# Leftover pairs of a two-layer expert product: weights of the first product held in the array, second product over half blocks

## The chip, the cores and the metric

The kernel runs on one core of a Trainium2 chip. A core has a matrix engine (TensorE, "PE"; its loads of the held operand are listed apart as "PEld"), a vector engine (VectorE, "DVE"), a scalar engine (ScalarE, "ACT"), GpSimd ("POOL") and a sync engine ("SP") that issues most DMAs. The metric is the device time of one execution in microseconds, the median of several. A "held" or "stationary" operand is the one a matmul loads into the array; the "moving" one streams past it.

## The reference, cut to what matters

An attention block makes 4608 token rows of 512 numbers, a dense gated layer maps each row to a new one, and then every token goes to one of 8 experts:

```python
logits = x @ w_gate                                  # x: (4608, 512)
e_idx = np.argmax(logits, axis=1)                    # one expert per token
eom = 1.0 / (1.0 + np.exp(-(x @ w_output_gate)))
for e in range(8):
    mask = e_idx == e
    h = np.maximum(x[mask] @ w1[e], 0.0)             # w1[e]: (512, 1024)
    ye = h @ w2[e]                                   # w2[e]: (1024, 512)
    out[mask] = gate_w[mask, None] * eom[mask, e, None] * ye
```

The change is in this last part alone, and there only in the tokens that are left over once whole blocks are taken.

## The kernel before, in words

The first 670 us compute the attention, the dense layer and the routing: rows are sorted by expert into a DRAM table `xs`, and a second table `tab` holds, for each sorted place, the token's number and its output factor. Then come two kinds of work, in an order written out by hand (`ORDER`):

- 16 **slots**. A slot takes up to 256 rows of one expert (`slot`, `gemm1`, `gemm2e`). Its products are made in three matmuls each from operands split into a rounded part and a rest, with the splitting on ACT (lines 1061, 1073) and DVE (1061, 1074). A slot's second products run one step late: they wait in `pend`, and `drain` issues them.
- **pairs**, for what is left. A pair takes two units of at most 64 rows each, mostly of two different experts, and works in unsplit float32. 11 pairs are in the program; three run always (before the sixth slot, before the tenth and at the end), and the eight behind them stand under nested conditions at the end, each taken only if there are that many units. With these inputs three run.

In a **pair** (line 1420), the two units share the array by column groups of 64: unit 0 uses columns 0 to 63 and PSUM partitions 0 to 63, unit 1 the others (`tile_position=(0, 64 * i)`). `pair1` (1028) holds the 64 rows of a unit, transposed, and streams 256 columns of its `w1` past them; a chunk is 4 such steps over the 512 inputs for each unit, and there are four chunks. Between chunk 0 and chunk 1 the last slot's waiting second products are issued (`drain(0)`). Two chunks fill one PSUM bank; ACT applies relu to it (`pair_relu`, 1036). The second product needs h with its features on the partitions, so `pair_turn` (1041) transposes it: four PE transposes by an identity (line 1044) into a PSUM bank, and a DVE copy (1046). `pair2` (1049) then holds 64 columns of the turned h and streams 512 columns of `w2`, eight steps for each unit. `finish` (1096) scales the bank on ACT (1104) and scatters its 128 rows of 2 KB to `out` with one indirect DMA issued by POOL (1107).

A float32 matmul of the program stands in the trace as two matmuls and two loads.

Weights come by DMAs that SP issues in program order (`load_weights`, 931): four of 512 KB for `w1` and four for `w2`, per unit or slot. SP has eight DMA semaphores which it uses in turn, so a DMA is issued once the one eight places earlier has landed. For slots and late pairs a DMA is skipped where the same expert's weights already lie there. `load_own` (959) fetches token numbers and factors, for a pair by two small DMAs.

Of the kernel before, what the change touches and what calls it, by code (L numbers as in the profile page):

```python
# [8 lines left out]
F32 = mybir.dt.float32  # L9
R32 = mybir.dt.float32r  # L10
B16 = mybir.dt.bfloat16
U32 = mybir.dt.uint32
AF = mybir.ActivationFunctionType
ALU = mybir.AluOpType
# [5 lines left out]
DM, DF = 512, 2048  # L20
NE, EF = 8, 1024
SEQ = NQ + NS
NX, NT = NB * NQ, NB * SEQ
# [59 lines left out]
def tile_kernel(  # L83
# [15 lines left out]
    nc = tc.nc  # L99
    V, S, G, T, D = nc.vector, nc.scalar, nc.gpsimd, nc.tensor, nc.sync  # L100
# [3 lines left out]
    def pool(c, name, bufs=1, side=None, space=None):  # L104
        kw = {"space": space} if space else {}
        return c.enter_context(tc.tile_pool(name=name, bufs=bufs, side=side, reuse_waits="tile", **kw))

    actx, nctx = ExitStack(), ExitStack()
    cp = pool(ctx, "cp", side="left")
    mp = pool(ctx, "mp", 2, side="left")  # L110
    wp = pool(nctx, "wp", side="left")
    np_ = pool(nctx, "np", side="left")
    ap = pool(actx, "ap", 2, side="right")
# [5 lines left out]
    tab = tc.dram_tile([NTAB, 2], U32, name="tab")  # L119
    half0 = tc.dram_tile([128, 4, DM], F32, name="half0")  # L120

    def psum(tag, bufs=1):
        return pp.tile([128, 512], F32, tag=tag, name=tag, bufs=bufs)

    ident = cp.tile([128, 128], F32, name="ident")
# [3 lines left out]
    def C(name):  # L129
        o, n = off[name]  # L130
        return cst[:, o:o + n]
# [6 lines left out]
    num, start = [cp.tile([128, 2 * NE], F32, name=t) for t in ("num", "start")]  # L138
    x1h = cp.tile([128, 4, 2 * 128], R32, name="x1h")
    x1l = cp.tile([128, 4, 2 * 128], R32, name="x1l")  # L140
    gap = cp.tile([128, 8], F32, name="gap")

    woh, wol = {}, {}
    win = [np_.tile([128, 4, 512], F32, name=f"win{c}") for c in range(4)]
# [3 lines left out]
    def not_yet(i):  # L148

        tc.add_manual_dep(i.ins, marks[-1].name, LATER, reason="has time")  # L150
# [396 lines left out]
    placed, put, first_placed, first_put = [], [], [], []  # L547

    sooner, later_rows = [], []

    def apart(i, mine, others):

        for o in others:
            tc.declare_no_dep(i, o, reason="rows of earlier batches")
        mine.append(i)

    def after(i, others):
        for o in others:
            tc.add_manual_dep(i, o.name, DEP, reason="token numbers in place")
# [364 lines left out]
    ws = {}  # L924

    def open_streams(qs, n0):
        for i in range(n0, n0 + 2):
            ws[i] = ([qs.tile([128, 4, 256], F32, name=f"w1s{i}{c}") for c in range(4)],
                     [qs.tile([128, 2, DM], F32, name=f"w2s{i}{c}") for c in range(4)])

    def load_weights(i, e_ap, need_ap):
        e = D.value_load(e_ap, min_val=0, max_val=NE - 1)
        kw = {}
        if need_ap is not None:
            kw["cond"] = D.value_load(need_ap, min_val=0, max_val=1)
        for k in range(2):
            for c in range(4):
                t = ws[i][k][c]
                src = (w1, w2)[k]
                D.dma_start(t.rearrange("p a f -> p (a f)"), src[bass.ds(e * 128, 128), 1024 * c:1024 * c + 1024], **kw)  # L940

    qa = {}
# [16 lines left out]
    def load_own(bases, n, placed):  # L959

        own = cp.tile([128, 2, 2], U32, tag="own", name="own", bufs=5)
        for j, reg in enumerate(bases):
            base = D.value_load(reg, min_val=0, max_val=NTAB - n)
            if n == 64:
                i = D.dma_start(own[64 * j:64 * j + 64, 0, :], tab[bass.ds(base, n), :]).ins
            else:
                i = D.dma_start(own, tab[bass.ds(base, n), :].rearrange("(t p) w -> p t w", p=128)).ins
            after(i, placed)
            if placed is first_placed:
                apart(i, sooner, later_rows)  # L970
        return own

    got_first, last_turned, last_w, evicted = [], [], [], []
# [29 lines left out]
        return xh, xl  # L1003

    zeros = {}

    def zero_tails(j0, j1):

        if j0 == 0:
            zeros["z"] = mp.tile([128, DM], F32, tag="xr", name="zeros", bufs=2)  # L1010
            V.memset(zeros["z"], 0.0)
            pair = carry.rearrange("p (j two) -> p two j", two=2)
            ends, zeros["at"] = one("ends", NE // 2), one("tails", NE // 2, U32)
            V.tensor_tensor(ends, pair[:, 1, :], pair[:, 0, :], op=ALU.subtract)
            V.scalar_tensor_tensor(ends, ends, C("half"), pair[:, 0, :], op0=ALU.mult, op1=ALU.add)
            V.tensor_scalar(zeros["at"], ends, C("part64"), None, op0=ALU.add)
        new = []
        for j in range(j0, j1):
            i = G.indirect_dma_start(xs, bass.IndirectOffsetOnAxis(ap=zeros["at"][:, j:j + 1], axis=0), zeros["z"], None).ins
            tc.add_manual_dep(i, last_w[0].name, DEP, reason="in its time")  # L1020
            apart(i, later_rows, sooner)
            for o in new:
                tc.declare_no_dep(i, o, reason="places are distinct")
            after(i, put)
            new.append(i)
        put.extend(new)

    def pair1(ps, c, x):

        for k in range(4):  # L1030
            for i in range(2):
                o = slice(64 * i, 64 * i + 64)
                T.matmul(ps[o, 256 * (c % 2):256 * (c % 2) + 256], x[:, k, o], ws[2 + i][0][c][:, k, :],
                         start=(k == 0), stop=(k == 3), tile_position=(0, 64 * i))

    def pair_relu(ps):
        h = mp.tile([128, 512], F32, tag="gh", name="hr", bufs=3)
        S.activation(h, ps, AF.Relu)
        return h

    def pair_turn(h):
        ps = psum("misc", 2)
        for k in range(4):
            T.transpose(ps[:, 128 * k:128 * k + 128], h[:, 128 * k:128 * k + 128], ident)
        hT = mp.tile([128, 4, 128], F32, tag="gl", name="hT", bufs=3)
        V.tensor_copy(hT.rearrange("p k t -> p (k t)"), ps)
        return hT

    def pair2(py, ft, hT):
        for i in range(2):  # L1050
            o = slice(64 * i, 64 * i + 64)
            T.matmul(py[o, :], hT[:, ft % 4, o], ws[2 + i][1][ft // 2][:, ft % 2, :], start=(ft == 0),
                     stop=(ft == 7), tile_position=(0, 64 * i))

    def gemm1(i, ft, xh, xl):
        w1t, w2t = ws[i]
# [34 lines left out]
            T.matmul(py[t], hl[:, sl], vh, start=False, stop=(ft == 7))  # L1091


    written = []

    def finish(py, ids, rows, quick=False):
        new = []
        ys = mp.tile([128, 2, DM], F32, tag="xr", name="y", bufs=2)
        for t in range(len(py)):
            y, gw = ys[:, t, :], ids[:, t, 1:2].bitcast(F32)  # L1100
            if quick and t:
                V.tensor_scalar(y, py[t], gw, None, op0=ALU.mult)
            else:
                i = S.activation(y, py[t], AF.Copy, scale=gw).ins
                for w in last_w[:1]:
                    tc.add_manual_dep(i, w.name, LATER, reason="the weights first")
            i = G.indirect_dma_start(rows, bass.IndirectOffsetOnAxis(ap=ids[:, t, 0:1], axis=0), y, None).ins  # L1107
            for o in new:
                tc.declare_no_dep(i, o, reason="a row is in one place")
            after(i, written)  # L1110
            new.append(i)
        written[:] = new
# [5 lines left out]
    rows = {0: attn_rows_first(0), 1: attn_rows(1)}  # L1118
# [16 lines left out]
    def more_start():  # L1135
        V.tensor_copy(carry, C("base"))
        V.tensor_copy(triu, C("tri"))
        V.memset(ones, 1.0)
        trow = mp.tile([128, DM], F32, tag="xr", name="trow", bufs=2)
        V.memset(trow, 0.0)  # L1140
        not_yet(D.dma_start(xs[TR:TR + 128, :], trow))
# [134 lines left out]
    for n, (b, f0, f1) in enumerate(segs[:-1]):  # L1276
# [4 lines left out]
        for ft in range(f0, f1):  # L1281
            h = h_xread(b, ft)
# [7 lines left out]
            if n >= 2 and ft == f0 + 2:  # L1290
                r = later.pop()
# [22 lines left out]
    got, turned, lists, owns = {}, {}, {}, {}  # L1314
# [76 lines left out]
    def bank():  # L1391
        banks[0] += 1
        return psum(f"o{(banks[0] - 1) % 4}")
# [26 lines left out]
    def pair(s):  # L1420
        j = ORDER[s][1]
        if s not in turned:
            turn_rows(s)
        x, _ = turned.pop(s)
        ps = psum("h", 2)
        pair1(ps, 0, x)
        drain(0)
        pair1(ps, 1, x)
        h = [pair_relu(ps)]
        ps = psum("h", 2)  # L1430
        pair1(ps, 2, x)
        hT = [pair_turn(h[0])]
        pair1(ps, 3, x)
        h.append(pair_relu(ps))
        py = bank()
        for ft in range(8):
            if ft == 2:
                hT.append(pair_turn(h[1]))
            if ft == 4:
                turn_next(s)  # L1440
            pair2(py, ft, hT[ft // 4])
        finish([py], owns.pop(s), out)
        if j + 1 < NP and j + 1 != CUT:
            fetch_pair(j + 1)

# [54 lines left out]
```

## Time and profile before

| | us |
|---|---|
| median of 3 runs (lowest to highest) | 1087.09 (1086.25 to 1089.58) |
| the profiled execution | 1088.14 |
| its span, first to last instruction | 1086.3 |
| PE busy | 1060.0 |
| PEld busy | 844.4 |
| DVE busy | 712.1 |
| ACT busy | 543.8 |
| POOL busy | 124.5 |

The span leaves out 1.84 us of the profiled execution. The granted TensorE clock was 0.999 of full speed over the span. PE is the engine that is hardly ever idle, so the places to look at are stretches in which PE works on the changed part, and the end of the span, where PE has finished and the last rows are still on their way out.

### The profile page before, as it was taken

Reading aid. Unit: us, or ns where it says so; the run is one execution under the profiler, and the core shown is the slowest. Engines: PE = TensorE matmul, PEld = TensorE weight load, DVE = VectorE, ACT = ScalarE, POOL = GpSimd, SP = SyncE. Lnnn points to the kernel's source line nnn. Section 1 sums busy time; section 2 is a strip of 40 time slices with the busy share of each in tenths; the row PEclk is TensorE's granted clock in tenths of the full one; section 3 lists DMA queues with packets and bytes.
Section 4 is the critical chain, followed back from the end, with each engine's and each line's share of the span. In section 5 each row is a group of like instructions: output and inputs, shape, how many; then the busy total and the mean of one; then the engine's idle time right before and its main releaser. Section 6 shows DMA issues by size and latency. Waiting matters only on the chain. (4 is left out here: it accounts for less than half of the span.)

```text
span 1086.3 us, 19260 instructions
## 1 busy us (share of the span) xinstructions
PE 1060.0 (98%) x6882; PEld 844.4 (78%) x6882; DVE 712.1 (66%) x1536; ACT 543.8 (50%) x1039; POOL 124.5 (11%) x138
## 2 busy tenths in 40 slices
PE   4999999999999999999999999999999999999997
PEld 1567777777777777777777899888869887998994
DVE  7997867845846747557455386986656665667761
ACT  4878834333434434334333345566545554566651
POOL 0000001221030020110300221220010010011001
PEclk9999999999999999999999999999999999999999
DMA  7646142642133223222130059576493879921500
GB/s 243 227 150 215 58 117 82 174 126 59 59 103 78 69 74 87 91 66 74 42 76 12 30 167 295 123 269 232 142 319 110 307 234 336 317 84 59 186 20 31
DMA packets 91237, 150.57 MB, mean 139 GB/s; under 512 B 20656, under 2 KB 59824, under 8 KB 91120
## 3 DMA queue, kind: packets, MB, share of 16 engines
q1 hardware_dynamic: 81760, 121.19, 35.8%
q0 software_dynamic: 9376, 28.09, 7.6%
q8 instruction: 56, 0.92, 0.4%
q14 instruction: 45, 0.37, 0.1%
HBM read 146.05 MB, written 29.68 MB: 162 GB/s over the span
## 5 line engine op out<-in xcount | busy, mean ns | idle before, releaser
L542 PE MATMUL o<-gh,wo 128*128 128x512 f32 x512 | 202.5, 396 | 0.0
L543 PE MATMUL o<-gh,wo 128*128 128x512 f32 x512 | 200.1, 391 | 0.2 <-DVE wo L809 0.2
L544 PE MATMUL o<-gl,wo 128*128 128x512 f32 x512 | 199.6, 390 | 0.0
L533 DVE SCALAR_TENSOR_TENSOR g<-r,h 128x512 f32<-128x512 f32 x128 | 87.3, 683 | 93.9 <-ACT r L532 93.7
L532 ACT ACTIVATE r<-h 128x512 f32<-128x512 f32 x128 | 76.3, 596 | 140.3 <-PE h L503 139.7
L534 ACT CAST gh<-g 128x512 fp32r<-128x512 f32 x128 | 79.4, 621 | 100.8 <-DVE g L533 99.9
L1074 DVE TENSOR_TENSOR vl<-w2s,vh 128x512 fp32r<-128x512 f32 x128 | 87.2, 684 | 55.3 <-ACT vh L1073 54.7
L535 DVE TENSOR_TENSOR gl<-g,gh 128x512 fp32r<-128x512 f32 x128 | 88.0, 688 | 47.5 <-ACT gh L534 47.0
L542 PEld LDWEIGHTS o<-gh,wo 128*128 128x128 f32 x512 | 96.1, 188 | 26.4 <-issue 5.9
L543 PEld LDWEIGHTS o<-gh,wo 128*128 128x128 f32 x512 | 96.1, 188 | 22.4 <-issue 1.7
L544 PEld LDWEIGHTS o<-gl,wo 128*128 128x128 f32 x512 | 96.1, 188 | 21.0 <-issue 1.0
L1073 ACT CAST vh<-w2s 128x512 fp32r<-128x512 f32 x128 | 79.0, 621 | 66.7 <-PE o L1091 57.2
L1091 PE MATMUL o<-vh,hl 128*128 128x512 f32 x256 | 100.2, 392 | 0.2 <-DVE hl L1078 0.2
L1090 PE MATMUL o<-vl,hh 128*128 128x512 f32 x256 | 100.4, 393 | 0.0
L503 PE MATMUL h<-ah,sh 128*128 128x512 f32 x240 | 97.6, 407 | 0.2 <-ACT ah L349 0.2
L1061 DVE TENSOR_TENSOR wl<-w1s,wh 128x512 fp32r<-128x512 f32 x128 | 86.3, 685 | 13.9 <-ACT wh L1061 9.9
L503 PE MATMUL h<-al,sh 128*128 128x512 f32 x240 | 93.8, 391 | 0.1
L503 PE MATMUL h<-ah,sl 128*128 128x512 f32 x240 | 93.4, 390 | 0.0
L1068 PEld LDWEIGHTS h<-xh,wh 128*128 128x128 f32 x512 | 77.0, 188 | 11.7 <-issue 1.6
L1068 PE MATMUL h<-xh,wh 128*128 128x256 f32 x512 | 81.9, 281 | 0.0
L1061 ACT CAST wh<-w1s 128x512 fp32r<-128x512 f32 x128 | 76.5, 619 | 10.4 <-PE h L1068 8.0
L1068 PE MATMUL h<-xh,wl 128*128 128x256 f32 x512 | 81.3, 279 | 0.1
(245 smaller groups left out, 1740.7 us busy)
## 6 DMA issues: line engine op xcount, KB each, us to landing
w1s<-w SPq DMA_DIRECT2D x88, 512.0 KB
w2s<-w SPq DMA_DIRECT2D x88, 512.0 KB
xd<-xr SPq DMA_DIRECT2D x68, 128.0 KB
xt<-xd POOLq DMA_DIRECT2D x17, 512.0 KB, 4.7
xT<-xT SPq DMA_DIRECT2D x16, 512.0 KB
wi<-w_in SPq DMA_DIRECT2D x16, 512.0 KB
wraw<-w_out SPq DMA_DIRECT2D x16, 512.0 KB
xq<-xq SPq DMA_DIRECT2D x16, 512.0 KB
```

Source lines behind the costliest of these rows:

```text
L503: T.matmul(ps, w[:, o:o + 128], a[:, e, :], start=(n == 0), stop=(n == 5))
L533: V.scalar_tensor_tensor(g6, r, 6.0, ps, op0=ALU.min, op1=ALU.mult)
L534: S.copy(gh, g6)
L535: V.tensor_tensor(gl, g6, gh.bitcast(F32), op=ALU.subtract)
L542: T.matmul(po[k][:, :n], woh[ft][:, s], gh, start=first, stop=False)
L543: T.matmul(po[k][:, :n], wol[ft][:, s], gh, start=False, stop=False)
L544: T.matmul(po[k][:, :n], woh[ft][:, s], gl, start=False, stop=last)
L1061: last_w[:] = [S.copy(wh, a).ins, V.tensor_tensor(wl, a, wh.bitcast(F32), op=ALU.subtract).ins]
L1068: T.matmul(ps, w[:, k, :], x[:, k, :], start=(m == 0), stop=(m == 11))
L1074: V.tensor_tensor(vl, c, vh.bitcast(F32), op=ALU.subtract)
L1090: T.matmul(py[t], hh[:, sl], vl, start=False, stop=False)
L1091: T.matmul(py[t], hl[:, sl], vh, start=False, stop=(ft == 7))
```

## The change

In a pair, `w1` becomes the held operand: 64 of its columns at a time, for unit 0 in column group 0 and for unit 1 in column group 1, while the unit's 64 token rows stream past. So h comes out with its features on the partitions, in blocks of 64 features, unit 0 on partitions 0 to 63 and unit 1 on 64 to 127, and nothing is transposed any more. The second product takes one block of 64 features per step, 16 steps: unit 0 uses rows 0 to 63 of the array and unit 1 rows 64 to 127, and each has its 512 output columns in two halves of 256, on the two column groups. So four matmuls of a step lie on four different quarters of the array, and each unit has a PSUM bank of its own. For that, `w2` of both units is loaded in half blocks, unit 0's to partitions 0 to 63 and unit 1's to 64 to 127 of one tile, by eight DMAs of 256 KB per unit instead of four of 512 KB. The scatter goes by half rows of 1 KB: one indirect DMA per unit, with row numbers 2·token + half that four small DVE instructions make. `load_own` reads a unit's table rows twice, once per half of the partitions. The output tensor has 128 more spare rows.

```diff
+    half_u = gap[:, 0:1].bitcast(U32)
     def open_streams(qs, n0):
+        both = [qs.tile([128, 4, DM], F32, name=f"w2p{c}") for c in range(4)] if n0 else None
...
-                     [qs.tile([128, 2, DM], F32, name=f"w2s{i}{c}") for c in range(4)])
+                     both or [qs.tile([128, 2, DM], F32, name=f"w2s{i}{c}") for c in range(4)])
     def load_weights(i, e_ap, need_ap):
...
+                if k and i > 1:
+                    o = 64 * (i - 2)
+                    for half in range(2):
+                        rows = src[bass.ds(e * 128 + 64 * half, 64), 1024 * c:1024 * c + 1024]
+                        D.dma_start(t[o:o + 64, half::2, :], rows.rearrange("q (f n) -> q f n", n=DM), **kw)
+                    continue
     def load_own(bases, n, placed):
...
-                i = D.dma_start(own[64 * j:64 * j + 64, 0, :], tab[bass.ds(base, n), :]).ins
+                new = [D.dma_start(own[o:o + 64, j, :], tab[bass.ds(base, n), :]).ins for o in (0, 64)]
     def pair1(ps, c, x):
-        for k in range(4):
-            for i in range(2):
-                o = slice(64 * i, 64 * i + 64)
-                T.matmul(ps[o, 256 * (c % 2):256 * (c % 2) + 256], x[:, k, o], ws[2 + i][0][c][:, k, :],
-                         start=(k == 0), stop=(k == 3), tile_position=(0, 64 * i))
+        for u in range(4):
+            n = 64 * (4 * (c % 2) + u)
+            for k in range(4):
+                for i in range(2):
+                    o = slice(64 * i, 64 * i + 64)
+                    T.matmul(ps[o, n:n + 64], ws[2 + i][0][c][:, k, 64 * u:64 * u + 64], x[:, k, o],
+                             start=(k == 0), stop=(k == 3), tile_position=(0, 64 * i))
-    def pair_turn(h):
...
-    def pair2(py, ft, hT):
+    def pair2(py, u, h):
         for i in range(2):
             o = slice(64 * i, 64 * i + 64)
-            T.matmul(py[o, :], hT[:, ft % 4, o], ws[2 + i][1][ft // 2][:, ft % 2, :], start=(ft == 0),
-                     stop=(ft == 7), tile_position=(0, 64 * i))
+            for c in range(2):
+                T.matmul(py[i][64 * c:64 * c + 64, 0:256], h[o, u % 8, :],
+                         ws[2][1][u // 4][o, u % 4, 256 * c:256 * c + 256], start=(u == 0), stop=(u == 15),
+                         tile_position=(64 * i, 64 * c))
+    halves_of_rows = out.rearrange("r (h n) -> (r h) n", h=2)
+    def finish_pair(py, ids):
+        new = []
+        ys = mp.tile([128, 4, 256], F32, tag="xr", name="y", bufs=2)
+        at = cp.tile([128, 2, 1], U32, tag="at2", name="at2", bufs=2)
+        for i in range(2):
+            V.scalar_tensor_tensor(at[:, i, :], ids[:, i, 0:1], 1, half_u, op0=ALU.logical_shift_left, op1=ALU.bitwise_or)
+        spare = cp.tile([128, 1], U32, tag="at3", name="spare", bufs=2)
+        V.tensor_scalar(spare, ids[:, 1, 0:1], NT, 256, op0=ALU.is_ge, op1=ALU.mult)
+        V.tensor_tensor(at[:, 1, :], at[:, 1, :], spare, op=ALU.add)
+        for i in range(2):
+            S.activation(ys[:, i, :], py[i][:, 0:256], AF.Copy, scale=ids[:, i, 1:2].bitcast(F32))
+            j = G.indirect_dma_start(halves_of_rows, bass.IndirectOffsetOnAxis(ap=at[:, i, :], axis=0), ys[:, i, :], None).ins
...
     def pair(s):
...
-        hT = [pair_turn(h[0])]
         pair1(ps, 3, x)
         h.append(pair_relu(ps))
-        py = bank()
-        for ft in range(8):
-            if ft == 2:
-                hT.append(pair_turn(h[1]))
-            if ft == 4:
+        py = [bank(), bank()]
+        for u in range(16):
+            if u == 8:
                 turn_next(s)
-            pair2(py, ft, hT[ft // 4])
-        finish([py], owns.pop(s), out)
+            pair2(py, u, h[u // 8])
+        finish_pair(py, owns.pop(s))
```

On PE, at the last pair, the rows before run from the end of the first product (line 1033) over the first steps of the second (1052); `w1s` and `w2s` are the weights, `xf` the token rows, `hT` the turned h:

```order
L1033 MATMUL h<-w1s_6960,xf 64x256
L1033 MATMUL h<-w1s_6968,xf 64x256
L1052 MATMUL o_12559<-w2s_6961,hT 64x512
L1052 MATMUL o_12559<-w2s_6969,hT 64x512
L1052 MATMUL o_12559<-w2s_6961,hT 64x512
L1052 MATMUL o_12559<-w2s_6969,hT 64x512
L1044 MATMUL misc<-ident,hr 128x128 x4
L1052 MATMUL o_12559<-w2s_6962,hT 64x512
L1052 MATMUL o_12559<-w2s_6970,hT 64x512
```

The same place of the changed kernel, whose lines are 1045 for the first product and 1057 for the second; `hr` is h as relu left it, and `w2p` the tile with `w2` of both units:

```order
L1045 MATMUL h<-xf,w1s_6965 64x64
L1045 MATMUL h<-xf,w1s_6969 64x64
L1057 MATMUL o_12953<-w2p_6958,hr 64x256 x2
L1057 MATMUL o_12954<-w2p_6958,hr 64x256 x2
L1057 MATMUL o_12953<-w2p_6958,hr 64x256 x2
L1057 MATMUL o_12954<-w2p_6958,hr 64x256 x2
```

The transposes are gone, the first product has 128 matmuls of 64 moving columns per pair in place of 32 of 256, and the second 64 of 256 in place of 16 of 512.

On DVE, at the first pair, the rows before copy the turned h, ahead of the next slot's weights (line 1061):

```order
L1078 SCALAR_TENSOR_TENSOR hl<-h,hh 128x256
L1001 TENSOR_TENSOR xl<-xt,xh 128x512 x2
L1074 TENSOR_TENSOR vl<-w2s_6139,vh 128x512 x2
L1046 COPY hT<-misc 128x512 x2
L1061 TENSOR_TENSOR wl<-w1s_6135,wh 128x512 x2
```

And the same place of the changed kernel, where lines 1068 to 1071 make the row numbers from `own` (1087 is the next slot's weights):

```order
L1104 SCALAR_TENSOR_TENSOR hl<-h,hh 128x256
L1010 TENSOR_TENSOR xl<-xt,xh 128x512 x2
L1100 TENSOR_TENSOR vl<-w2s_6140,vh 128x512 x2
L1068 SCALAR_TENSOR_TENSOR at_9051<-own,gap 128x1 x2
L1070 TENSOR_SCALAR spare<-own 128x1
L1071 ISA at_9051<-at_9051,spare 128x2
L1087 TENSOR_TENSOR wl<-w1s_6136,wh 128x512 x2
```

Two copies that waited for PE have gone, and four small instructions stand there that wait for the table rows in `own`.

## Rows read from the trace of the kernel before

**Rows 1.** The page, span and busy time of each engine.
```profile
span 1086.3 us, 19260 instructions
...
PE 1060.0 (98%) x6882; PEld 844.4 (78%) x6882; DVE 712.1 (66%) x1536; ACT 543.8 (50%) x1039; POOL 124.5 (11%) x138
```

**Rows 2.** Waits of PE, 690 to 1087 us: total, times, longest in us.
```profile
PE o L1091 <- DVE hl L1078: 0.2, 1, 0.2
```

**Rows 3.** Stretches of first and last pair: length, busy of each engine (instructions), clock, DMA.
```profile
783.94:801.08 17.14, 17.14 (x112) 8.43 (x111) 4.91 (x8) 4.72 (x9) 1.93 (x2) 1.00 0.76 246
...
1062.80:1080.00 17.20, 17.20 (x111) 8.43 (x110) 1.38 (x2) 2.46 (x4) 1.92 (x2) 1.00 0.09 33
```

**Rows 4.** Timeline of PE, last pair: start, length, engine, line, what, count.
```profile
1062.80 1.95 PE L1033 MATMUL h<-w1s,xf 128*64 128x256 f32 x16
1064.68 0.73 PE L1087 MATMUL o<-vh,hh 128*128 128x512 f32 x2
...
1066.26 3.67 PE L1033 MATMUL h<-w1s,xf 128*64 128x256 f32 x32
1069.87 0.66 PE L1044 MATMUL misc<-ident,hr 128*128 128x128 f32 x4
1070.45 1.95 PE L1033 MATMUL h<-w1s,xf 128*64 128x256 f32 x16
1072.23 1.89 PE L1052 MATMUL o<-w2s,hT 128*64 128x512 f32 x8
1074.05 0.66 PE L1044 MATMUL misc<-ident,hr 128*128 128x128 f32 x4
1074.63 5.37 PE L1052 MATMUL o<-w2s,hT 128*64 128x512 f32 x24
```

**Rows 5.** By line, the pairs' first product: least, median, greatest ns.
```profile
L1033 PE MATMUL h<-w1s,xf x192: 379/379/430, 783.9 to 1072.0; 128*64 128x256 f32 x192
```

**Rows 6.** Timelines: four 32-column tiles; 128-column loads; eight 64-row tiles.
```profile
224.09 1.10 PE L427 MATMUL h<-xq,a2T 128*32 128x64 f32 x64
...
1060.39 0.63 PE L1068 MATMUL h<-xl,wh 128*128 128x256 f32 x4
...
324.84 1.09 PE L237 MATMUL misc<-win,st 64*32 64x512 f32 x16
```

**Rows 7.** By line, the matmuls of the first two of these.
```profile
L427 PE MATMUL h<-xq,a2T x320: 219/219/243, 224.1 to 520.4; 128*32 128x64 f32 x160
...
L1068 PE MATMUL h<-xh,wh x512: 277/280/390, 671.5 to 1060.3; 128*128 128x256 f32 x171
```

**Rows 8.** Timeline of POOL and ACT at the end: last slot's and last pair's output.
```profile
1066.87 0.96 POOL L1107 DMA_INDIRECT out<-y,own  x1 [20.59 <-ACT y L1104]
1068.14 0.96 POOL L1107 DMA_INDIRECT out<-y,own  x1 [0.31 <-issue]
...
1080.08 0.69 ACT L1104 ACTIVATE y<-o,own 128x512 f32<-128x512 f32 x1 [7.01 <-PE o L1052]
...
1081.04 0.96 POOL L1107 DMA_INDIRECT out<-y,own  x1 [11.95 <-ACT y L1104]
```

**Rows 9.** By line and shape, from 700 us: ACT evicting 256 columns.
```profile
L1077 ACT ACTIVATE hh<-h 128x256 fp32r<-128x256 f32 x118 | 45.1, 382 | 49.5 <-PE h L1068 48.7
```

**Rows 10.** Timeline of SP: first pair's weights begin; a later slot's weights.
```profile
716.34 2.15 SPq L940 DMA_DIRECT2D w1s<-w  x4
...
752.17 2.49 SPq L940 DMA_DIRECT2D w1s<-w  x4
```

**Rows 11.** Timeline: that slot's first weights cast on ACT, and used on PE.
```profile
757.86 1.13 ACT L1061 CAST wh<-w1s 128x512 fp32r<-128x512 f32 x2
...
761.55 0.63 PE L1068 MATMUL h<-xh,wh 128*128 128x256 f32 x4
```

**Rows 12.** The stretch ahead of that slot's weights, columns as in Rows 3.
```profile
744.00:752.00 8.00, 8.00 (x49) 7.04 (x49) 7.80 (x17) 6.64 (x14) 0.00 (x0) 1.00 0.18 51
```

**Rows 13.** The page, the DMA queue of instructions: packets, MB, share of 16 engines.
```profile
q8 instruction: 56, 0.92, 0.4%
```

More of the change, by code (lines that the diff above doesn't have):

```diff
@@ L964, in load_own @@
             if n == 64:
-                i = D.dma_start(own[64 * j:64 * j + 64, 0, :], tab[bass.ds(base, n), :]).ins
+                new = [D.dma_start(own[o:o + 64, j, :], tab[bass.ds(base, n), :]).ins for o in (0, 64)]
             else:
[L967 to L970, printed above, removed]
+                new = [D.dma_start(own, tab[bass.ds(base, n), :].rearrange("(t p) w -> p t w", p=128)).ins]
+            for i in new:
+                after(i, placed)
+                if placed is first_placed:
+                    apart(i, sooner, later_rows)
         return own
@@ L1005, in tile_kernel @@
     zeros = {}
+    written = []
     def zero_tails(j0, j1):
@@ L1036, in pair_relu @@
     def pair_relu(ps):
-        h = mp.tile([128, 512], F32, tag="gh", name="hr", bufs=3)
-        S.activation(h, ps, AF.Relu)
-        return h
-    def pair_turn(h):
[L1042 to L1047, printed above, removed]
-    def pair2(py, ft, hT):
+        h = mp.tile([128, 8, 64], F32, tag="gh", name="hr", bufs=3)
@@ L1050, in pair2 @@
+        S.activation(h.rearrange("p u t -> p (u t)"), ps, AF.Relu)
+        return h
+    def pair2(py, u, h):
         for i in range(2):
             o = slice(64 * i, 64 * i + 64)
-            T.matmul(py[o, :], hT[:, ft % 4, o], ws[2 + i][1][ft // 2][:, ft % 2, :], start=(ft == 0),
-                     stop=(ft == 7), tile_position=(0, 64 * i))
+            for c in range(2):
+                T.matmul(py[i][64 * c:64 * c + 64, 0:256], h[o, u % 8, :],
+                         ws[2][1][u // 4][o, u % 4, 256 * c:256 * c + 256], start=(u == 0), stop=(u == 15),
+                         tile_position=(64 * i, 64 * c))
@@ new lines, in tile_kernel @@
+    halves_of_rows = out.rearrange("r (h n) -> (r h) n", h=2)
[11 more added lines that the diff above has]
+            j = G.indirect_dma_start(halves_of_rows, bass.IndirectOffsetOnAxis(ap=at[:, i, :], axis=0), ys[:, i, :], None).ins
+            for o in new:
+                tc.declare_no_dep(j, o, reason="a row is in one place")
+            after(j, written)
+            new.append(j)
+        written[:] = new
@@ L1091, in gemm2e @@
             T.matmul(py[t], hl[:, sl], vh, start=False, stop=(ft == 7))
-    written = []
     def finish(py, ids, rows, quick=False):
@@ L1138, in more_start @@
         V.memset(ones, 1.0)
+        V.tensor_copy(half_u, C("half"))
         trow = mp.tile([128, DM], F32, tag="xr", name="trow", bufs=2)
@@ L1493 @@
     args[3], args[4] = args[3].bitcast(U32), args[4].bitcast(U32)
-    out = nc.dram_tensor("out", (NT + 128, DM), F32, kind="ExternalOutput").ap()
+    out = nc.dram_tensor("out", (NT + 256, DM), F32, kind="ExternalOutput").ap()
     with tile.TileContext(nc) as tc:
```

## The prediction

> **What bounds the kernel now.** I read the page first: PE is busy in 1060.0 of the 1086.3 us of the span, 98% [rows 1]. The waits of PE say whether that busy time is also the path. From 690 us to the end, where the slots and pairs lie, it waits for another engine once, for 0.2 us [rows 2]. So a nanosecond taken from PE inside a pair comes off the end, and so does one added; what the other engines do costs nothing until it makes PE wait. The windows then give the piece that is changed: PE is busy in all of the 17.14 us of the first pair and the 17.20 of the last, at a granted clock of 1.00 [rows 3]. Three pairs run, so a change of d in a pair is worth 3d.
>
> The timeline of PE cuts a pair into its parts [rows 4]. The first product takes 1.88 (1062.80 to 1064.68), 3.61 (1066.26 to 1069.87) and 1.78 us (1070.45 to 1072.23), in all 7.27. The slot's waiting second products between them take 1.58 (1064.68 to 1066.26) and are not touched. The transposes take 2 x 0.58 = 1.16. The second product takes 1.82 and, by its last piece, 5.37, in all 7.19. The sum is 17.20. (A piece's own length overlaps the next start, so I take starts, and the length only for the last.)
>
> **First product.** Before, a pair has 64 matmuls in the trace's count, 32 groups of two that share the array, and each streams 256 columns. From the first two pieces, which differ by 8 groups, a group takes (3.61 - 1.88)/8 = 0.216 us, and the ends of the three pieces 7.27 - 32 x 0.216 = 0.36. After, a group streams 64 columns and there are four times as many: 128 groups of two, and 256 loads of 64 columns. The streamed columns of a column group are as many as before, so the question is only whether such a group can start every 216/4 = 54 ns while its two loads are made beside it. The trace has no matmul of this shape, so I bound the period of a group from rows:
>
> - From above: the first product's matmuls last 379 ns, and the longest 430 [rows 5]; the 51 ns more I take for a load of 64 columns that isn't hidden, on top of the period with hidden loads.
> - From below: line 427 holds 128 rows by 32 columns and streams 64 columns past four column groups; 64 of its matmuls take 1.10 us [rows 6], the length of one being 0.219 [rows 7]. So (1.10 - 0.22)/63 = 14 ns per matmul and 56 ns per group of four. It loads 128 columns in that time, as a group here would. The upper bound is then 56 + 51 = 107 ns.
> - Between them: line 1068 holds 128 columns and streams 256. Four take 0.63 us [rows 6] and one lasts 280 ns, the longest 390 [rows 7], so (0.63 - 0.28)/3 = 117 ns a matmul, where by the same reading a load takes 390 - 280 = 110. So matmuls follow each other at a load and 7 ns; for 64 columns in a column group of its own that is 51 + 7 = 58 ns.
>
> I take 58, by the row whose loads are as long as its matmuls, beside line 427, which is the nearest in the length that moves: 128 x 0.058 = 7.42, with the same 0.36 for the ends 7.78 us, 0.51 more than before. With 56 it is 7.53.
>
> [...]
>
> **Transposes.** Four PE transposes go twice: -1.16 us. The DVE copies behind them go as well, and PE no longer needs them between the products. What is late in their place is relu: the second product's first eight steps read the first relu's half, made two chunks earlier, and the last eight read the second relu's, which starts when the first product ends. Eight steps take 3.5 us (below) and an ACT pass over 512 columns 0.69 [rows 8], so it is covered fivefold.
>
> **Second product.** Before, a matmul of 512 columns on each of two column groups, 16 groups in the trace's count, 7.19/16 = 0.45 each. After, 32 groups of four matmuls of 256 columns on four quarters of the array. If the four go together, a group takes what 256 columns took in the first product, 0.216 us: 32 x 0.216 and 0.22 for the ends, as long as one matmul of line 427, are 7.13, 0.06 less than before. The trace shows such sharing on tiles of 64 rows by 32 columns: 16 matmuls of 512 columns in 1.09 us [rows 6], where one after another would take 16 x 0.43 = 6.9. From above, two at a time, it is 64 x 0.216 + 0.22 = 14.0 us. I take the lower end, since the row has the same kind of tile.
>
> A pair then is 7.78 + 1.58 + 7.13 = 16.49 us, 0.71 less than 17.20, and three pairs give -2.1 us.
>
> **The end of the span.** Here ACT and POOL lie on the path. Before, one eviction of 512 columns takes 0.69 (1080.08) and one scatter's issue 0.96 (1081.04) [rows 8]. After, two evictions of 256 columns, 0.38 each [rows 9], and two scatters. The first scatter can start 0.3 us earlier; the second begins 1.27 after the first, as the two of the slot did (1066.87 and 1068.14) [rows 8]. So the last scatter starts 1.27 - 0.31 = 0.96 us later than now, and its landing with it. That rows go as halves of 1 KB I cost at nothing, since the last scatter has half the bytes; from -0.3 to +0.3, as much as the first scatter is early. In the other two pairs the second scatter lies in POOL's idle time, 12 to 20 us before each issue [rows 8].
>
> **Edits off the path.** The four DVE instructions on row numbers wait for `own`; behind them in DVE's queue stand the next slot's `wl`. They are one to two columns wide, each shorter than the copy of 512 columns that left; DVE is busy in 4.9 of the first pair's 17.1 us [rows 3]. An integer addition of this kind isn't in the trace: between nothing and 3 us, of which the idle 12 hide all. The two evictions cost ACT 0.08 more; ACT is busy 4.7 of 17.1 us there. Both lie on PE's path only if PE waits for them.
>
> The weights: per pair eight more DMAs for `w2` on SP and two more for `own`, each 0.5 to 0.6 us of SP's time (2.15 for four, 2.49 for four) [rows 10], so some 6 us of SP per pair. SP also waits for the DMA eight places earlier, and now eight DMAs are 2 MB instead of 4. The nearest point is a later slot's weights, issued from 752.17 [rows 10], cast from 757.86 and used at 761.55 [rows 11]. Cast to use is 3.7 us, of which the casts take 1.1 and more, so some 2 to 3 us of delay pass unseen. Before it, the DMA moves 51 GB/s where the first pair's stretch had 246 [rows 12, 3]: there is room on the wires. I expect the new pattern to delay these loads by about 1 us, which the slack hides; if it is 6 (all of SP's new time at this one place), PE waits 3 to 4.
>
> **Sum.** -2.1 + 0.96 = -1.2 us on the profiled execution's 1088.14 (span and the 1.84 around it): 1086.9. That execution lies 1.05 above the median of the runs, 1087.09, so the median comes to 1085.9. A difference of 0.3%, 3.3 us, is about what a measurement can tell from no change. So the forecast is: no change that can be told.
>
> **The rivals.**
>
> A, slower: loads of 64 columns are not hidden. Place: line 1045. The first product takes 128 x 0.107 + 0.36 = 14.1 instead of 7.78, a pair 22.8, which is 5.6 more than before; 3 x 5.6 + 0.96 = +17.7, so 1104.8. It decides from the period: up to 58 + 0.71/0.128 = 63.5 ns the pair still gains, and at 70 ns the three pairs and the end together are 3.3 us slower. For it: the 51 ns [rows 5]. Against: line 427 [rows 6]. Chance 0.10.
>
> B, slower: PE runs out of instructions. PE has 2 x 6882 = 13764 records [rows 1], and the queue that brings instructions 56 packets [rows 13], on average 246 records a packet. A packet takes 0.4% of 16 x 1086.3 us over 56, 1.24 us. The new first product has 512 records in 7.4 us, two packets' worth; a pair three. If each is waited for in full, 9 x 1.24 = 11.2, and with the -1.2 the time is 1097.1. For it: no stretch of several us in the trace has had such small matmuls in such number. Against: line 427 has 128 records in 1.1 us without a wait. A lesser wait, 0.5 us a packet, brings 4.5 - 1.2 = +3.3 and is the point from which it shows. Chance 0.10.
>
> C, slower: DMAs to 64 partitions run at half the rate. At a DMA share of 0.76 the first pair's stretch had 246 GB/s [rows 3], so 324 at a full one, by which the 4.2 MB of a pair's `w2` take 13 us; at half the rate they take 13 more, the slot's weights behind them come 13 - 3 = 10 us late, and the time is 1087.1 - 1.2 + 10 = 1095.9. For it: half the partitions in each DMA. Against: eight may be in flight, and both halves are. Chance 0.06.
>
> D, slower: two of the four quarters at a time. The second product takes 6.9 us more, 3 x 6.9 - 1.2 = +19.5, so 1106.6. Against: line 237 [rows 6]. Chance 0.05.
>
> E, faster by over 0.3%: the pair gains more than the sum. With 56 ns it gains 0.25 more in each pair, -1.9 in all; it needs another 1.4 us, such as a scatter that lands sooner or a neighbour that starts earlier, and comes to 1083.5 or so. Chance 0.08.
>
> The forecast has the other 0.61.
>
> **How the numbers follow.** The likeliest's own range is 1084.9 to 1088.5: 56 ns at one end, and a delay at that later slot of up to 2.6 us past its cover at the other. The range for 8 in 10 leaves out A and D (0.15) and a little of E: 1083.5, about 3.6 below the median, to 1097.5, which takes in C and B at their full price. Faster by over 0.3% is E, 0.08. Slower by over 0.3% is A, C, D and B from its point on (0.08 of 0.10): 0.29. Within 0.3% is the rest, 0.63.
>
> **What would show it.** The first product's matmuls (line 1045): two every 56 to 58 ns for this forecast, every 107 for A. Line 1057: four every 0.216 us, or every 0.43 for D. The stretch of a pair: 16.5 us. PE's waits in the pairs: none; "issue" gaps inside line 1045 for B; a wait for a slot's weights some 25 us after the first pair's loads for C. The last scatter: about 1 us further behind PE's end than before. The forecast is wrong if a pair is not 16 to 17 us, or if PE waits for more than 1 us in all after 690 us.

## The result: 1.3% slower, and the profile after

The changed kernel takes 1102.92 us (median of 5 runs, 1101.73 to 1103.91). The kernel before, timed again beside it, takes 1088.47, so the ratio is 1.0133 (95% interval 1.0122 to 1.0145). The forecast was 1085.9 with a range of 1083.5 to 1097.5. Two counts in the description above are wrong: the rows are 4352, not 4608, and nine pairs are in the program, six of them under conditions, not eleven and eight.

The page of the changed kernel, its span and busy times (of before: [rows 1]):

```profile
span 1102.1 us, 21040 instructions
...
PE 1063.3 (96%) x7722; PEld 863.4 (78%) x7722; DVE 709.1 (64%) x1543; ACT 543.9 (49%) x1042; POOL 127.2 (12%) x141
```

PE is busy 3.3 us more, but the span is 15.8 us longer: most of the time is lost where PE stands still. Its waits from 690 us on, total, times, longest (of before: [rows 2]):

```profile
PE h L1094 <- ACT wh L1087: 8.8, 1, 8.8
PE o L1117 <- DVE hl L1104: 0.2, 1, 0.2
```

One wait of 8.8 us, at the first product of a slot (line 1094), for weights that ACT has not cast. SP's timeline shows why (start, length, what, count):

```profile
719.04 1.99 SPq L948 DMA_DIRECT2D w1s<-w  x4
721.24 8.00 SPq L946 DMA_DIRECT2D w2p<-w  x8
730.38 3.77 SPq L948 DMA_DIRECT2D w1s<-w  x4
735.03 14.38 SPq L946 DMA_DIRECT2D w2p<-w  x8
750.93 2.72 SPq L948 DMA_DIRECT2D w1s<-w  x4
754.29 1.98 SPq L948 DMA_DIRECT2D w2s<-w  x4
```

These are the first pair's weights, unit 0 and unit 1 (719.04 to 749.4), and behind them a slot's (750.93). The same slot's weights in the kernel before:

```profile
734.05 4.52 SPq L940 DMA_DIRECT2D w1s<-w  x4
739.67 3.93 SPq L940 DMA_DIRECT2D w2s<-w  x4
```

and the use of that slot's first weights there, on PE:

```profile
740.05 0.63 PE L1068 MATMUL h<-xh,wh 128*128 128x256 f32 x4
```

The slot's DMAs are skipped in both kernels, since that expert's weights already lie there. By line, in the changed kernel, SP's time for each DMA (least, median, greatest ns), for the pair's first `w1` and then for the slot's:

```profile
L948 SPq DMA_DIRECT2D w1s<-w x4: 332/345/358, 719.0 to 720.7; - x4
L948 SPq DMA_DIRECT2D w1s<-w x4: 73/78/93, 750.9 to 753.6; - x4
```

But a skipped DMA still takes its turn on the eight semaphores, and so waits for the pair's weights to land: these four start over 2.7 us, though each takes under 0.1, and SP waits 1.4 us of it for `w2p` to land. ACT casts as soon as it has passed, and PE begins 0.7 us later:

```profile
751.02 0.62 ACT L1087 CAST wh<-w1s 128x512 fp32r<-128x512 f32 x1 [10.44 <-DMA w1s<-w]
751.70 1.22 PE L1094 MATMUL h<-xh,wh 128*128 128x256 f32 x4 [8.78 <-ACT wh L1087]
```

Three windows of the changed kernel, then one of before (columns as in [rows 3]):

```profile
734.00:738.00 4.00, 4.00 (x28) 3.61 (x27) 1.86 (x4) 1.39 (x3) 0.00 (x0) 1.00 1.07 212
738.00:742.00 4.00, 4.00 (x25) 3.54 (x24) 1.37 (x3) 1.00 (x2) 0.00 (x0) 1.00 1.01 368
746.00:750.00 4.00, 0.00 (x0) 0.00 (x0) 0.00 (x0) 0.00 (x0) 0.00 (x0) 0.50 1.06 205
```

```profile
734.00:738.00 4.00, 4.00 (x27) 3.62 (x27) 1.86 (x4) 1.50 (x4) 0.00 (x0) 1.00 1.02 406
```

The DMA engines are full in all four, but in the first and third, where `w2` of a unit goes to 64 partitions, they move 212 and 205 GB/s in place of 406. Between them it is 368: there, by the order of issue, the second unit's `w1` is on its way, to all 128 partitions. The granted clock is 0.50 in the third: PE, idle since 742.91, restarts at 0.50 (four matmuls take 1.22 us for 0.63) and loses another 1.4 us until about 755.

The pairs themselves came out as forecast, the second 0.3 us longer than the others. Their windows (of before: [rows 3]):

```profile
797.02:813.44 16.42, 16.42 (x392) 13.47 (x391) 3.97 (x10) 4.81 (x9) 1.93 (x2) 1.00 0.79 236
901.99:918.81 16.82, 16.82 (x391) 15.20 (x391) 3.98 (x10) 5.11 (x10) 2.06 (x2) 1.00 0.92 272
1074.79:1091.28 16.49, 16.49 (x391) 13.47 (x390) 0.00 (x0) 2.46 (x4) 1.91 (x2) 1.00 0.10 35
```

PE's timeline of the last (of before: [rows 4]):

```profile
1074.79 2.08 PE L1045 MATMUL h<-xf,w1s 128*64 128x64 f32 x64
...
1078.39 5.82 PE L1045 MATMUL h<-xf,w1s 128*64 128x64 f32 x192
1084.14 7.14 PE L1057 MATMUL o<-w2p,hr 64*64 64x256 f32 x128
```

With a matmul's 0.22 us taken off, (5.82 - 0.22)/191 = 29.3 ns, 58.6 per group of two; 58 was taken. The second product takes 7.14; 7.13 was forecast.

The end, in POOL's timeline (of before: [rows 8]):

```profile
1092.06 0.96 POOL L1074 DMA_INDIRECT out<-y,at  x1 [10.85 <-ACT y L1073]
1093.32 0.96 POOL L1074 DMA_INDIRECT out<-y,at  x1 [0.30 <-issue]
```

and, by line, the semaphore work behind it (least, median, greatest ns, first and last start; in before it stood at 1081.8):

```profile
L1481 POOLq INC_SWDGE_SEM  x1: 916/916/916, 1097.3 to 1097.3; - x1
```

Before, that work began 0.8 us after the last scatter, now 4.0. From PE's last matmul to the end it is 10.8 us, 6.3 before.

The sum, from the starts of the same matmuls in the two traces: +2.7 us up to the slot at 740, +8.95 by the wait, +1.4 by the low clock behind it, -0.7, -0.3 and -0.7 in the pairs, +4.5 at the end: +15.8, the two spans' difference.

### The profile page after: what moved, and what is told of

Its sections match the earlier page's. It is cut to its first block, busy times and chain, and to the rows that moved or that the text cites. A ratio compares the mean times of both kernels' runs of the same rounds, so it can differ in the third digit from the quotient of the medians.

```text
span 1102.1 us, 21040 instructions
## 1 busy us (share of the span) xinstructions
PE 1063.3 (96%) x7722; PEld 863.4 (78%) x7722; DVE 709.1 (64%) x1543; ACT 543.9 (49%) x1042; POOL 127.2 (12%) x141
## 5 line engine op out<-in xcount | busy, mean ns | idle before, releaser
L544 PEld LDWEIGHTS o<-gh,wo 128*128 128x128 f32 x512 | 96.5, 188 | 23.3 <-issue 1.9
```

The source lines that it names most:

```text
L544: T.matmul(po[k][:, :n], wol[ft][:, s], gh, start=False, stop=False)
```

## The experiments

Before was timed anew in each group (1089.8 to 1090.3 us), so the ratios are what compares.

**What made the weights late.** e1_w2_128:

```diff
-    rows = src[bass.ds(e * 128 + 64 * half, 64), 1024 * c:1024 * c + 1024]
-    D.dma_start(t[o:o + 64, half::2, :], rows.rearrange("q (f n) -> q f n", n=DM), **kw)
+    rows = src[bass.ds(e * 128, 128), 1024 * c + DM * half:1024 * c + DM * half + DM]
+    D.dma_start(t[:, 2 * (i - 2) + half, :], rows, **kw)
```

> The changed kernel, but each of the sixteen w2 DMAs of a pair's two units goes to all 128 partitions in pieces of 2 KB instead of 64 partitions (so the products read rows that don't belong to them; the work is the same). Bytes, number of DMAs, size of the pieces and everything else stay. Theory 'half the partitions': between 730 and 750 us the DMA engines were at a share of 1.06 with 205 to 256 GB/s, where before they moved 406 to 424 at 1.02, because 64 partitions take half the rate; here the rate comes back, the slot behind the first pair gets its weights some 14 us earlier, PE's wait of 8.8 us and the 1.3 us of low clock behind it go: about 1092.8. Theory 'small pieces' (2 KB instead of 4 KB) and theory 'more DMAs over eight semaphores': nothing changes, 1102.9.

Measured: 1097.77 us, ratio 1.0075 (1.0056 to 1.0095). Its windows in the same place, and its waits of PE:

```profile
734.00:738.00 4.00, 4.00 (x29) 3.70 (x29) 1.81 (x3) 1.44 (x4) 0.00 (x0) 1.00 1.03 422
738.00:742.00 4.00, 4.00 (x25) 3.53 (x24) 1.55 (x3) 1.25 (x3) 0.00 (x0) 1.00 1.04 398
```

```profile
PE h L1045 <- issue: 1.5, 4, 0.4
PE o L1117 <- DVE hl L1104: 0.7, 1, 0.7
```

The rate is back and the wait gone, with as many DMAs and pieces of the same size. The slot's first `w1` still passes 23.3 us after the pair's first weight, where before has 17.7: 5.5 us of delay come with the number and size of the DMAs and their pieces alone, about as much as the slot has in hand. It stays 0.75%, some 8 us, above before: about 5 at the end, 2.3 by addresses, and gaps in the pairs beyond their gain, all of them below.

e2_w2_4k:

```diff
-    D.dma_start(t[o:o + 64, half::2, :], rows.rearrange("q (f n) -> q f n", n=DM), **kw)
+    D.dma_start(t[o:o + 64, 2 * half:2 * half + 2, :].rearrange("p f n -> p (f n)"), rows, **kw)
```

> The changed kernel, but the w2 DMAs put 4 KB in one piece on each of the 64 partitions instead of two pieces of 2 KB (the order of the blocks in the tile changes, and the second product reads them in that order). Bytes, number of DMAs and partitions stay. 'Small pieces': the wait of 8.8 us goes, 1092.8. 'Half the partitions' and 'more DMAs': 1102.9 as before, PE's wait 8 to 10 us.

Measured: 1106.97 us, ratio 1.0147 (1.0130 to 1.0164); PE waits 6.9 us, and the DMA rate stays low:

```profile
746.00:750.00 4.00, 0.00 (x0) 0.00 (x0) 0.00 (x0) 0.00 (x0) 0.00 (x0) 0.52 1.03 207
```

The size of the pieces isn't it.

e11_w2_512:

```diff
-    for half in range(2): ...
+    rows = src[bass.ds(e * 128, 128), 1024 * c:1024 * c + 1024]
+    D.dma_start(t[o:o + 64].rearrange("q (h f) n -> q h (f n)", h=2),
+                rows.rearrange("(h q) m -> q h m", h=2), **kw)
```

> The changed kernel with each unit's w2 in four DMAs of 512 KB to 64 partitions, two pieces of 4 KB each, instead of eight of 256 KB. In the runs so far the stretch from the first weight of the first pair to the first of the slot behind it is 17.5 us (128 partitions, DMAs of 512 KB), 23.3 (128 partitions, 256 KB), 30.5 to 31.9 (64 partitions, 256 KB). If number and half partitions add up, it falls to about 25 here and the slot waits about 1 to 2 us instead of 8: ratio about 1.008. If with 64 partitions the transfers themselves are the bound, it stays at 30 and so does the ratio of 1.015.

Measured: 1106.81 us, ratio 1.0150 (1.0131 to 1.0169). With half as many DMAs the slot's `w1` does pass at 21.8 us, but its `w2` only at 32.1, and the wait moves there:

```profile
PE o L1113 <- ACT vh L1099: 5.4, 2, 3.3
```

So fewer DMAs gain nothing in the time; my sum of the two shares was wrong, the transfers are the bound. Each of these DMAs reads 128 rows of `w2`, as those of before do, and still 219 GB/s is all that moves from 734 to 738 us: what counts is the 64 partitions written, not the rows read.

e6_halves, on the kernel before:

```diff
+    if k and i > 1:
+        for o in (0, 64):
+            D.dma_start(t[o:o + 64].rearrange("p a f -> p (a f)"),
+                        src[bass.ds(e * 128 + o, 64), 1024 * c:1024 * c + 1024], **kw)
+        continue
```

> The kernel before, but each w2 DMA of a pair goes as two, partitions 0 to 63 and 64 to 127, 4 KB per partition, one behind the other. The products, the tail and all else are those of before. Theory 'a transfer to 64 partitions is slow by itself': w2 takes as long as in the change, the slot behind the first pair waits 6 to 9 us, about +8 us. Theory 'slow only because those in flight together go to the same half': here neighbours go to different halves, the rate stays near 420 GB/s, and the time is that of before within 2 us, since 5 us of delay are covered at the slot.

Measured: 1096.05 us, ratio 1.0047 (1.0031 to 1.0063), with a wait of 5.0 us at the same slot in the profile. (That execution, 1100.38 us, is the longest of the four; it is 5.3 us behind before already when PE reaches 720 us, ahead of the edited DMAs.) This one edit brings the wait into the kernel before, against "only the same half".

e7_alt: the changed kernel's `fetch_pair` issues `w1` of both units, then

```diff
+    for c in range(4):
+        for half in range(2):
+            for i in range(2):
+                rows = w2[bass.ds(e[i] * 128 + 64 * half, 64), 1024 * c:1024 * c + 1024]
+                D.dma_start(ws[2][1][c][64 * i:64 * i + 64, half::2, :], rows.rearrange(...), **kw[i])
```

> The changed kernel, but a pair's loads go in another order: w1 of both units, then w2 of both units by turns, a DMA to partitions 0 to 63 and one to 64 to 127, and so on; same DMAs, same sizes. If only transfers to the same half at the same time hold each other up, the wait of 7 to 9 us at the slot goes or falls under 2 us and the ratio to before falls from 1.013 to about 1.005. If each such transfer is slow by itself, it stays at 1.013.

Measured: 1108.66 us, ratio 1.0173 (1.0153 to 1.0192). The wait falls to 4.1 us, but the median doesn't move; its second pair takes 19.5 us, with a further gap of 1 us. Turns help the transfer a little (248 to 254 GB/s from 738 to 750 us), not the time. Beside each other (us from the pair's first weight to the slot's first `w1` and first `w2`, by SP's timelines):

| kernel | partitions, KB per DMA of w2 | to w1 | to w2 | PE's wait | ratio |
|---|---|---|---|---|---|
| before | 128, 512 | 17.7 | 23.3 | 0 | 1 |
| e1_w2_128 | 128, 256 | 23.3 | 25.0 | 0 | 1.0075 |
| e6_halves (on before) | 64 by turns, 256 | 28.8 | 31.0 | 5.0 | 1.0047 |
| e7_alt | 64 by turns, 256 | 27.2 | 30.2 | 4.1 | 1.0173 |
| e11_w2_512 | 64, 512 | 21.8 | 32.1 | 5.4 | 1.0150 |
| e2_w2_4k | 64, 256 in 4 KB pieces | 30.5 | 34.1 | 6.9 | 1.0147 |
| changed kernel | 64, 256 in 2 KB pieces | 31.9 | 35.3 | 8.8 | 1.0133 |

**The end.** e3_one_cond:

```diff
+            if one and i:
+                continue
             j = G.indirect_dma_start(halves_of_rows, ...)
```

Here `one` is true for the pairs under a condition.

> The changed kernel, but the six pairs under conditions, which do not run with these inputs, have one scatter each instead of two (their second is left out). Theory 'skipped branches': at the end POOL passes the skipped pairs' blocks, and there waits for each DMA semaphore that their scatters use; with twelve these are all eight, the last scatter's among them, so 0.9 us of semaphore work and a drain of 3.0 us stand behind its landing at 1097.1; with six they run beside it, and the end comes 3 us earlier: 1099.9. Theory 'half rows land late' (128 pieces of 1 KB): the landing is the same 3.8 us after the issue and the end stays, 1102.9.

Measured: 1105.56 us, ratio 1.0141 (1.0126 to 1.0157); beside e2_w2_4k and e5_again (1.0147, 1.0163) the times alone don't tell. The trace does, in POOL's timeline and by line:

```profile
1096.84 0.96 POOL L1076 DMA_INDIRECT out<-y,at  x1 [0.30 <-issue]
```

```profile
L1483 POOLq INC_SWDGE_SEM  x1: 930/930/930, 1096.9 to 1096.9; - x1
```

The semaphore work begins with the last scatter, not behind its landing. From PE's end it is 8.65 us, where the seven profiles with twelve scatters have 10.7 to 11.6. That is at least 2.1 us, not 3: what is left over 6.3 is the second scatter's 1.0 and a landing that comes 4.3 us after its start, not 2.7 as before. Why it lands later no run shows.

**The pairs.** e4_cross, on the kernel before, without the transposes:

```diff
+        for u in range(4):
+            n = 128 * (2 * (c % 2) + u // 2)
+            for k in range(4):
+                for i in range(2):
+                    b = u ^ i
+                    g = 64 * (b % 2)
+                    T.matmul(ps[g:g + 64, n + 64 * i:n + 64 * i + 64], ws[2 + i][0][c][:, k, 64 * b:64 * b + 64],
+                             x[:, k, 64 * i:64 * i + 64], start=(k == 0), stop=(k == 3), tile_position=(0, g))
...
-            pair2(py, ft, hT[ft // 4])
+            pair2(py, ft, h[ft // 4])
```

> The kernel before with w1 held as in the change, but with the blocks of 64 features crossed: in a step, unit 0's even block goes to one column group and unit 1's odd block to the other, next step the other way round, so each unit's h lies with 128 features on 128 partitions. The second product, w2's loads, the table rows and the scatter are those of before; only the transposes and their copies are gone. If the pair's working is right (first product 7.8 instead of 7.27, transposes 1.16 gone) a pair takes 16.5 us and the time is 2 us below before, about 1086.4, with no wait at the slot and the end of before. Rival: crossing the groups makes the loads follow one another (107 ns per two matmuls), a pair is 22.8 and the time 1105.

Measured: 1090.10 us beside 1090.30, ratio 1.0003 (0.9994 to 1.0012). No wait at the slot and an end of 6.24 us, as expected; yet no gain. Its second and third pairs take longer than the 16.4 to 16.8 of the changed kernel:

```profile
889.67:907.41 17.74, 16.95 (x295) 11.95 (x294) 3.62 (x6) 4.82 (x9) 2.06 (x2) 1.00 0.83 263
1063.37:1081.02 17.65, 17.02 (x295) 11.95 (x294) 0.00 (x0) 2.46 (x4) 1.92 (x2) 1.00 0.09 33
```

PE is idle in them for 0.8 and 0.6 us, with "issue" as the reason, in two gaps each inside the first product.

e5_again (no edit):

> The changed kernel once more, unaltered, beside the next three. Its ratio to before should be 1.013 again, with PE's wait for the slot's weights of 7 to 9 us. Open is whether its pairs have the stalls of about 0.6 us inside the first product that the four kernels run since have (two each in the second and third pair, which made them 17.7 to 18.0 us long) and that the first profile of this kernel lacks (16.4 to 16.8). Theory 'instructions arrive late, by how the execution falls': it has them this time, or some of them. Theory 'the edits of those four kernels brought them': it has none.

Measured: 1108.64 us, ratio 1.0163 (1.0144 to 1.0182). Its pairs take 17.04, 18.10 and 17.95 us; the second, in PE's timeline:

```profile
907.06 2.27 PE L1045 MATMUL h<-xf,w1s 128*64 128x64 f32 x57
909.75 0.34 PE L1045 MATMUL h<-xf,w1s 128*64 128x64 f32 x3 [0.41 <-issue]
910.47 4.09 PE L1045 MATMUL h<-xf,w1s 128*64 128x64 f32 x132 [0.38 <-issue]
```

So the same program has the gaps here and lacked them in the first profile: 3.4 us over three pairs, twice the 1.7 that the pairs had gained. All later profiles with this first product at its full rate have them, on three chips; which chip the first ran on isn't known, so execution and chip aren't told apart.

e8_spread, against e4_cross:

```diff
         pair1(ps, 2, x)
+        py = bank()
+        for ft in range(2):
+            pair2(py, ft, h[0])
         pair1(ps, 3, x)
```

> The crossed kernel with two of the eight steps of the second product moved ahead of the last chunk of the first product, so that the long run of small matmuls (three chunks, 384 records of matmuls and as many loads) is broken. If the stalls of 0.6 us come from instructions arriving late after a long dense run, one of the two per pair goes: about 1 to 1.5 us less than the crossed kernel, 0.999 of before. If they come within the first two chunks, they stay, and the time is that of before, ratio 1.000.

Measured: 1091.09 us, ratio 1.0007 (0.9996 to 1.0018). The pairs take 16.6, 17.8 and 17.7 us: the gaps lie in the first three chunks, ahead of what was moved.

e12_wide, against e4_cross:

```diff
-    T.matmul(ps[g:g + 64, n + 64 * i:n + 64 * i + 64], ..., x[:, k, 64 * i:64 * i + 64], ...)
+    T.matmul(ps[g:g + 64, n:n + 128], ..., x[:, k, 0:128], ...)
```

> The crossed kernel whose first product streams the 128 token rows of both units past each unit's weights instead of its own 64 (the result of the pairs is wrong; instructions are as many, each streams twice the columns). Without stalls its first product takes twice the 7.4 us of streaming, a pair about 24. If the stalls of 0.6 us come from the number of instructions in a given time, at half the rate there is none in these pairs. If they come at fixed places in the code, whatever the rate, there are again two of 0.6 us in the second and third pair.

Measured: 1108.07 us in one run. Its second pair:

```profile
898.39:921.14 22.75, 22.75 (x296) 17.44 (x295) 3.62 (x6) 4.82 (x9) 2.06 (x2) 1.00 0.66 204
```

No gap in any pair (22.7 to 22.8 us), with the same instructions at half the rate. That fits gaps which depend on the rate, but it is one execution, and the first profile of the changed kernel had none at the full rate. That it is the supply of instructions fits as well, but no row shows what PE waits for, so this stays open.

**The untouched part.** e9_shift, on the kernel before:

```diff
+    cp.tile([128, 32], F32, name="shim")
     first = NA + CUT
```

> The kernel before with nothing but an unused tile of 128 bytes per partition among the constants, as much as the change's row numbers take there: all tiles that lie above on the left side move up by 128 bytes, those on the right side stay. In all profiles of the changed kernel's family the untouched part from 180 to 670 us is 0.5% longer, 2.5 to 3 us in all, by 4 to 5 ns at some changes of operand. Theory 'addresses': here too, ratio 1.0025 (+2.7 us), and no other difference. Theory 'something else of the change (its instructions, its code)': ratio 1.000.

Measured: 1092.00 us, ratio 1.0021 (1.0010 to 1.0031). Nothing but addresses differs. The matmuls of the attention part with the operands `ah` and `sl`, 200 to 660 us (columns: count, busy us, mean ns), in before and then in e9_shift:

```profile
L503 PE MATMUL h<-ah,sl 128*128 128x512 f32 x182 | 70.9, 390 | 0.0
```

```profile
L503 PE MATMUL h<-ah,sl 128*128 128x512 f32 x182 | 71.5, 393 | 0.0
```

e10_noshift, on the changed kernel:

```diff
-        own = cp.tile([128, 2, 2], U32, tag="own", name="own", bufs=5)
+        own = cp.tile([128, 2, 4], U32, tag="own", name="own", bufs=5)
...
-        at = cp.tile([128, 2, 1], U32, tag="at2", name="at2", bufs=2)
+        at = ids[:, :, 2:3]
```

> The changed kernel with its row numbers kept in unused words of the table-row tile, so that no tile of the first part lies elsewhere than before. 'Addresses': the untouched part to 670 us is as long as in the kernel before, 2.5 to 3 us less than the changed kernel, ratio 1.0137 where that has 1.0163 beside the last runs; the slot's wait, the stalls in the pairs and the end stay. 'Something else': ratio 1.0163.

Measured: 1106.05 us, ratio 1.0146 (1.0128 to 1.0164); alone that doesn't part it from 1.0163. In its trace the same row is that of before again, where e5_again has 71.5:

```profile
L504 PE MATMUL h<-ah,sl 128*128 128x512 f32 x182 | 70.9, 390 | 0.0
```

From 180 to 720 us its matmuls fall 0.3 us behind those of before, in e5_again 2.7, in e9_shift 2.4. In the first profile it is 2.0 from 180 to 650 us; the rest of its +2.7 up to the slot is a step of 1.4 near 670 us, which e5_again and e9_shift don't have, and -0.7 elsewhere.

## Why the prediction was wrong

- **The pair's sum was right in the first profile**: first product 58.6 ns per group for 58, second product 7.14 for 7.13, pairs of 16.4 to 16.8 for 16.5. Rivals A and D did not happen.
- **The step that failed is the one on the weights**: "I expect the new pattern to delay these loads by about 1 us, which the slack hides". The delay was 14.2 us (31.9 from the pair's first weight to the slot's, for 17.7). Two errors lie in it. I took the slot at 752 as the nearest point and overlooked the one at 734.05, directly behind the pair's weights, whose DMAs are skipped but still wait their turn; its cover was 5.3 us, from 734.05 to the use at 740.05 less the 0.7 of the cast, and 14.2 - 5.3 is the wait. And I priced the loads by SP's time, not by what the transfers take: of the 14.2 us, 5.5 come with sixteen smaller DMAs in place of eight (e1) and the other 8.6 with half the partitions. Rival C named the cause, and with 0.06 far too small a chance: e1, e2 and e11 part the partitions from the rest, and e6 brings the wait into the kernel before. In windows of 4 us with a unit's `w2` on its way to 64 partitions, as the first and third above, 205 to 219 GB/s moved (the changed kernel, e2, e11), with 128 partitions 398 to 424 (before, e1). Why half the partitions move at half the rate no run shows. That rival C's 13 us lie so near the 14.2 is partly luck, since it left the 5.5 out.
- **The end was mis-sized**: +4.5 us for +0.96. The second scatter's own 1.0 was right. Missed was that twelve scatters in skipped branches make POOL wait for the last landing before its closing work (2.1 us or more by e3), and that the second landing is slower (3.8 us after its start, 4.3 in e3, for 2.7 before), where the half rows were costed at nothing; why it is slower stays open.
- **Not in the sum at all**: tiles moved by 128 bytes, which costs some 2 us in the untouched part (e9, e10), and PE's clock of 0.50 after the wait, 1.4.
- **Rival B half came true**: no gaps in the first profile, 3.4 us in e5_again. As it was put, that each packet of instructions is waited for, isn't shown.

None of the versions beats the kernel before. The crossed one equals it: it avoids the loads, the second scatter and the shift, and its pairs give back what the transposes cost whenever the gaps come.

## What to carry to other kernels

When a change halves the partitions that a DMA writes, price it at half the rate (205 to 219 GB/s for 398 to 424 here), price more and smaller DMAs too, and look for the first consumer queued behind it, skipped DMAs included. Lay blocks so that each transfer still fills all partitions, as crossing the column groups does here. And before counting a gain of 0.2%, see whether new small tiles moved the addresses of everything behind them, and what a closing branch waits for.

## What was not expected of the hardware

- Moving a part of the tiles by 128 bytes changes matmul time (e9): where `ah`/`sl` matmuls are followed by those of `gh`/`wo`, starts are 232 ns apart (median) instead of 227; 0.5% of the attention part. Whether the address counts or the distance between operands, no run shows.
- The same program has gaps in one execution and none in another, in stretches with a matmul every 29 ns: about 0.6 us from one start to the next, two each in the second and third pair.
- DMAs by turns to the two halves of the partitions win back little: in DMAs of 256 KB the slot's `w1` passes after 27 to 29 us, with 128 partitions after 23, with one half at a time after 30 to 32.
